# Group 9's gate logits as PE products, and the first slot's gathers behind that group's row store

## The chip, the cores and the metric

The kernel runs on one core of one Trainium2 chip. The metric is the device time of one execution in microseconds (us), the median of three runs; a profiled execution, from which the rows below come, is timed apart from these.

## What is computed

The reference has three stages. The first is a recurrent attention over 4 batches, 8 heads, 768 steps and a head size of 40:

```python
y[:, :, t] = np.einsum('bhd,bhde->bhe', rt, state)
Sa = np.einsum('bhde,bhe->bhd', state, at)
state = state * wt[:, :, None, :] - np.einsum('bhd,bhe->bhde', Sa, bt) + np.einsum('bhd,bhe->bhde', vt, kt)
```

Its result, 3072 tokens of 320 features, goes through a dense layer pair (320 to 2048 and back, with a leaky ReLU of slope 0.01). The last stage sends each token to one of 8 experts: the largest of 8 gate logits picks the expert, its softmax probability scales the result, and the expert is again a layer pair, 320 to 1024 and back with a ReLU. All is float32.

## The kernel before, in words

The attention is computed in 24 chunks of 32 steps. Two chunks of all batches make a group of 256 tokens, so there are 12 groups (0 to 11), and the dense layers work group by group behind the attention. A group has 16 steps, one for each 128 of the 2048 inner features, and each step is done in two halves: a call of `half` runs either layer 1 of a step (eight products into psH, line 716) or layer 2 of the step two before it (six products into psX, line 732). After layer 1 ScalarE (ACT) writes 0.01 of it to g (L720), VectorE (DVE) takes the maximum (L721), ACT rounds it to gh (L722), and GpSimd (POOL) subtracts to get the rest, gl (L723); layer 2 multiplies gh and gl. g has two buffers, gh and gl have three each.

When a group's layer 2 is complete, `route` (line 734) makes a list of pieces. The first, `take` (L750), copies the two token tiles (128 tokens each) from psX to the tile X, which has one buffer. From then on every call of `half` does one piece after its products. There are two forms of the logits. Groups below TURNED (line 36) take one DVE instruction for each expert and tile, 16 in all (L753, with weights in raws). From TURNED on a tile is transposed by TensorE (PE) in three pieces (`turn`, L759), copied by ACT (L760), multiplied by the gate weights on PE (`product`, L765) and copied by ACT again (L766); both tiles take 6 pieces. Then follow the maximum, the expert's code and the denominator (L772 to L793), the row store of X to the DRAM tensor x2d by SyncE (SP) (`fourth`, L797: two DMAs, of 128 rows with 385 numbers each), and two scatters of token numbers into a table by POOL (L810). A group's store comes 23 pieces after the first logit in the DVE form and 15 after it in the PE form. Some of a route's pieces do nothing, to keep a distance.

When the routes of group 8 and of group 9 are through, `early` (line 920) works out on DVE which experts have the fullest slots of 256 tokens: slots 0 and 1 after group 8, slot 2 after group 9 (EARLY, line 38). `fetch` (line 1055) then reads a slot's token numbers from the table (SP, L1063), adds two halves (POOL, L1070) and gathers the tokens' rows from x2d with two indirect DMAs on POOL (L1071) into xg. Loads of an expert's weights are five DMAs of SP into raw (L1049), which ACT and DVE split into two parts (L1091, L1092).

The kernel is scheduled by hand: each engine takes its instructions in the order in which the code emits them. Two strings of words set that order, one word for one thing to emit. The attention's strings end with the 336th call of `half`, 16 halves into group 10. From there the string TAIL (line 61) rules, read by `tail` (line 1422): H is one half of the dense layers with its routing piece, l one weight load, s one piece of the split, i the reads of the table for slots 0 and 1, t one step of their fetch (clearing xg, first gather, second gather, then the same for slot 1), x the transposes of slot 0. The framework puts a wait where two instructions touch the same tile or the same DRAM tensor; x2d counts as one tensor for gathers and stores alike.

Group 9's copy into X is in half 324 and its first logit piece too; group 10's copy is in half 356. TAIL's first H is half 337.

Of the kernel before, what the change touches and what calls it, by code (L numbers as in the profile page):

```python
# [22 lines left out]
B, H, S, D = 4, 8, 768, 40  # L23
# [9 lines left out]
CAP = NT + SL  # L33
NSLOT = NT // SL + E - 1
PACE = (2, 1), (2, 2), (2, 2)
TURNED = 10
FETCH = 1, 5
EARLY, NE = {9: (0, 1), 10: (2,)}, 3
LOAD, SPLIT = 18, 27
# [19 lines left out]
    "H H s1 H s2 w w H H H w H s6a.-1 s6b.-1 w s3x H H s3a w H s4a s4b H w H s5a s5b w l3.1 H H s3b H l2.1 H H w w H "  # L59
)  # L60
TAIL = (
    "i H l t H H H H t l l H t l H H H l H s H H H H H H s H H H H H H s H H t H H H t H t H H c s s H H H H s H H l H H H H H H H H s H H H s x s H l H l H "
    "l s l H H "
)
NFIX = NT // SL + E // 2
NTB = 8 * CAP + 8 * SL
# [439 lines left out]
class Moe1:  # L506
# [313 lines left out]
    def units(s):  # L820
# [3 lines left out]
        def second():  # L824
            g, f, gh, gl = lag.pop(0)
            s.layer2(f, gh, gl)
            if f == NF - 1:
                r = s.route([s.x2c[2 * g], s.x2c[2 * g + 1]], s.ids[:, 2 * g:2 * g + 2], g >= TURNED)
                r.pop(0)()
# [625 lines left out]
```

## Time and profile before

| what | us |
|---|---|
| median of three runs | 1109.37 |
| the runs | 1102.41, 1109.37, 1110.74 |
| profiled execution, its own time | 1101.14 |
| its span, first to last instruction | 1099.4 |
| PE busy in the span | 948.1 (86%) |
| DVE busy | 803.1 (73%) |
| ACT busy | 529.3 (48%) |
| POOL busy | 501.1 (46%) |
| mean granted clock of PE | 0.955 |

The span is cut by three stages: attention and dense layers together up to some 761 us, dense layers alone up to some 826 us, then the experts. PE is TensorE's products, PEld its weight loads. A row of the timeline gives the start, the busy time, the engine, the line, the operation with output and inputs, and in brackets how long the engine had been idle and what ended that. A row of waits gives who waited for whom, the total, how often, and the longest. In the tables of stretches each engine has its busy time and its count, then come the granted clock as a share of full speed, the busy share of the DMA engines and their GB/s.

### The profile page before, as it was taken

The page shows a single profiled execution, that of the slowest core. Times are in us where ns is not written, and L with a number is a line of the kernel's source. Part 1 is how long each engine was busy: PE and PEld are TensorE (multiplying, and loading weights), DVE is VectorE, ACT ScalarE, POOL GpSimd, SP SyncE. Part 2 cuts the span into 40 slices and gives each one's busy share as a digit, 9 for nine tenths or more (in the row PEclk, how much of TensorE's full clock was granted, in tenths as well). Part 3 has the DMA queues.
Part 4 walks back from the last instruction along what each step waited for, and adds up shares of the span by engine and source line. Part 5 has one row for each costly group of instructions (what it writes and reads, how often), then busy time and mean ns, then how long its engine had stood idle before and what let it go on. Part 6 is the DMA issues. An engine that isn't in the chain of part 4 may idle for free. (4 is left out here: it accounts for less than half of the span.)

```text
span 1099.4 us, 40716 instructions
## 1 busy us (share of the span) xinstructions
PE 948.1 (86%) x16853; PEld 893.9 (81%) x16853; DVE 803.1 (73%) x1882; ACT 529.3 (48%) x1316; POOL 501.1 (46%) x690
## 2 busy tenths in 40 slices
PE   3476788978899988889989999999798899999993
PEld 3366677768788887888889988998798899999993
DVE  8989787757778787868787767667447777777761
ACT  4545554653434444444435443444456466666650
POOL 5124145214873489447864595334456333233210
PEclk9999986878999999999999999999899999999997
DMA  7978776846445755564555432331425663732520
GB/s 249 241 223 224 213 209 177 222 132 194 134 123 161 163 158 160 163 167 125 151 150 151 117 81 81 82 91 48 149 87 159 168 178 111 236 109 70 173 91 17
DMA packets 132523, 163.20 MB, mean 148 GB/s; under 512 B 67851, under 2 KB 90011, under 8 KB 132199
## 3 DMA queue, kind: packets, MB, share of 16 engines
q1 hardware_dynamic: 122215, 141.31, 46.3%
q10 hardware_dynamic: 5760, 10.49, 3.3%
q0 software_dynamic: 4352, 8.69, 2.7%
q8 instruction: 135, 2.21, 0.9%
q14 instruction: 61, 0.50, 0.2%
HBM read 127.62 MB, written 42.27 MB: 155 GB/s over the span
## 5 line engine op out<-in xcount | busy, mean ns | idle before, releaser
L723 POOL TENSOR_TENSOR gl<-g,gh 128x256 fp32r<-128x256 f32 x192 | 155.3, 812 | 227.9 <-ACT gh L722 202.1
L721 DVE TENSOR_TENSOR g<-psH,g 128x256 f32<-128x256 f32 x192 | 81.1, 423 | 119.2 <-ACT g L720 117.5
L722 ACT CAST gh<-g 128x256 fp32r<-128x256 f32 x192 | 77.9, 406 | 166.3 <-DVE g L721 163.2
L732 PE MATMUL psX<-woh,gh 128*128 128x320 f32 x384 | 133.9, 349 | 2.0 <-ACT woh L643 1.1
L732 PE MATMUL psX<-woh,gl 128*128 128x320 f32 x384 | 124.2, 323 | 6.0 <-POOL gl L723 5.8
L720 ACT ACTIVATE g<-psH 128x256 f32<-128x256 f32 x192 | 73.5, 383 | 112.4 <-PE psH L716 87.5
L732 PE MATMUL psX<-wol,gh 128*128 128x320 f32 x384 | 123.2, 321 | 0.0
L264 PE MATMUL psA<-AtI,KB 40*64 40x72 f32 x1408 | 71.0, 264 | 34.7 <-DVE KB L243 18.5
L264 PEld LDWEIGHTS psA<-AtI,KB 40*64 40x64 f32 x1408 | 62.8, 166 | 41.1 <-POOL woh L242 18.5
L753 DVE SCALAR_TENSOR_TENSOR junk<-X,raws 128x320 bf16<-128x320 f32 x160 | 92.1, 576 | 5.0 <-ACT X L750 3.1
L716 PE MATMUL psH<-xh,wih 128*128 128x256 f32 x384 | 86.3, 308 | 4.4 <-DVE g L721 3.6
L732 PEld LDWEIGHTS psX<-woh,gl 128*128 128x128 f32 x384 | 76.1, 198 | 9.0 <-POOL gl L723 8.8
L304 POOL TENSOR_TENSOR itmp<-Tinv 128x30 f32<-128x30 f32 (+14 forms) x120 | 71.0, 592 | 25.4 <-DVE Tinv L296 18.2
L732 PEld LDWEIGHTS psX<-woh,gh 128*128 128x128 f32 x384 | 76.3, 199 | 7.5 <-ACT woh L643 1.3
L716 PE MATMUL psH<-xl,wih 128*128 128x256 f32 x384 | 80.6, 293 | 0.0
L716 PE MATMUL psH<-xh,wil 128*128 128x256 f32 x384 | 80.2, 292 | 0.0
L1155 POOL DMA_INDIRECT out<-ey,sid x32 | 32.4, 1011 | 105.0 <-ACT ey L1154 99.5
L732 PEld LDWEIGHTS psX<-wol,gh 128*128 128x128 f32 x384 | 76.7, 200 | 0.5 <-DVE wol L644 0.3
L310 POOL TENSOR_TENSOR Tinv<-Tinv,itmp 128x30 f32<-128x30 f32 (+14 forms) x120 | 71.8, 598 | 7.8
L716 PEld LDWEIGHTS psH<-xh,wih 128*128 128x128 f32 x384 | 65.9, 199 | 8.9 <-DVE g L721 5.5
L1133 DVE SCALAR_TENSOR_TENSOR ehl<-psH,ehh 128x256 fp32r<-128x256 f32 x86 | 36.2, 421 | 41.5 <-ACT ehh L1132 41.3
L1132 ACT ACTIVATE ehh<-psH 128x256 fp32r<-128x256 f32 x86 | 33.1, 384 | 64.9 <-PE psH L1129 62.7
(284 smaller groups left out, 2792.3 us busy)
## 6 DMA issues: line engine op xcount, KB each, us to landing
raw<-hwe SPq DMA_DIRECT2D x48, 512.0 KB
raw<-hwe SPq DMA_DIRECT2D x32, 640.0 KB
in<-h SPq DMA_DIRECT2D x23, 521.0 KB
KB<-h SPq DMA_DIRECT2D x22, 512.0 KB
L<-dKBr SPq DMA_DIRECT2D x24, 320.0 KB
dKBr<-KBr SPq DMA_DIRECT2D x22, 320.0 KB
lamY<-dl SPq DMA_DIRECT2D x24, 264.0 KB
dl<-lam SPq DMA_DIRECT2D x22, 264.0 KB
```

What stands on the lines that cost most here:

```text
L264: nc.tensor.matmul(v[64 * i:64 * i + 64, k, :], z["KB"][64 * i:64 * i + 40, p, :], z["AtI"][64 * i:64 * i + 40, p, :], start=True, stop=True)
L304: eng.tensor_tensor(out=box["v"], in0=T[:, k + 1:32, k:k + 1].to_broadcast([128, n, k]), in1=T[:, k:k + 1, 0:k].to_broadcast([128, n, k]), ...
L310: eng.tensor_tensor(out=T[:, k + 1:32, 0:k], in0=T[:, k + 1:32, 0:k], in1=box["v"], op=ALU.add)
L716: nc.tensor.matmul(ps[:, 0:256], w, x, start=(n == 0), stop=(n == 7))
L720: nc.scalar.activation(out=g, in_=ps[:, 0:256], func=AF.Copy, scale=0.01)
L721: nc.vector.tensor_tensor(out=g, in0=ps[:, 0:256], in1=g, op=ALU.max)
L722: nc.scalar.copy(out=gh, in_=g)
L723: return gh, gl, lambda: nc.gpsimd.tensor_tensor(out=gl, in0=g, in1=gh, op=ALU.subtract)
L732: nc.tensor.matmul(s.x2[t][:, 0:DM], x[:, o], w[:, f, :], start=(f == 0 and n == 0), stop=(f == NF - 1 and n == 2))
L753: nc.vector.scalar_tensor_tensor(out=s.junk, in0=X[:, t, 0:DM], scalar=1.0, in1=s.wg[:, e], op0=ALU.mult, op1=ALU.mult, accum_out=lg[:, t, ...
L1132: nc.scalar.activation(out=hh, in_=ps, func=AF.Relu)
L1133: nc.vector.scalar_tensor_tensor(out=hl, in0=ps, scalar=0.0, in1=hh, op0=ALU.max, op1=ALU.subtract)
```

## The change

Two constants change; no function does.

```diff
-TURNED = 10
+TURNED = 9
 TAIL = (
-    "i H l t H H H H t l l H t l H H H l H s H H H H H H s ...
+    "i H l t H H H H l l H l H H t H H t l s H H H H H H s ...
...
-    "l s l H H "
+    "l H l s l H H "
```

The strings break at another place, so that a word has gone from the end of the one line to the start of the next; all words behind the second gather (the third t) keep their order, as do the counts of H, l, s and t. With TURNED at 9 group 9 uses the PE form. Its route is 8 pieces shorter: the store is emitted with half 339 (347 before), the scatters with halves 340 and 343 (348 and 351), and the work of `early` for slot 2 with half 343 (351). The two gathers of slot 0 come after halves 344 and 346 (341 and 342 before). So they stood ahead of group 9's store and now stand behind it, by 5 and 7 halves, or by 8 and 10 words of TAIL that are not t.

On PE the transposes of group 9's first tile come in at half 324, behind the group's last layer-2 products (psX) and ahead of the next layer-1 products (psH); X is the tile that ACT copies from psX.

```order
 L732 MATMUL psX_12816<-wol,gh 128x320
 L732 MATMUL psX_12816<-woh,gl 128x320
+L759 MATMUL psA<-ident,X_13678 128x128 x3
 L716 MATMUL psH<-xh,wih 128x256 x2
 L716 MATMUL psH<-xh,wis 128x256
```

One row is new here, and the layer-1 products of the next step stand behind it.

On SP this is the place from group 11's input (xl) to the first expert's weights (raw); X_13678 is group 9's X.

```order
 L693 DMA xl<-xT_88 64x256
 L694 DMA xl<-xT_88 64x256
+L797 DMA x2d<-X_13678 4x32x385 x2
 L1049 ISA
 L1049 DMA raw<-hwe 128x1024
```

The store stood behind the four weight loads that follow here, next to group 10's store, and is now ahead of them.

On POOL this is the stretch from the clearing of slot 0's xg to that of slot 1's; tbl_90 and tbl_91 are the two halves of the table.

```order
 L1075 MEMSET xg 128x770
 L723 TENSOR_TENSOR gl<-g,gh 128x256 x2
-L1070 TENSOR_TENSOR sid<-sid_14024 128x2
+L810 DMA tbl_90<-ids,dst 28672x1
+L723 TENSOR_TENSOR gl<-g,gh 128x256
+L810 DMA tbl_91<-ids,dst 28672x1
+L723 TENSOR_TENSOR gl<-g,gh 128x256
+L1070 TENSOR_TENSOR sid<-sid_14037 128x2
 L1071 DMA xg<-x2d,sid 128x385
 L723 TENSOR_TENSOR gl<-g,gh 128x256
 L1071 DMA xg<-x2d,sid 128x385
```

The scatters of group 9 were behind the gathers and are ahead of them; two more subtractions gl come ahead of the first gather.

## Rows read from the trace of the kernel before

**Rows 1.** Busy time by stretch: us, then PE, PEld, DVE, ACT, POOL, clock, DMA, GB/s.

```profile
700.00:750.00 50.00, 50.00 (x1058) 46.78 (x1057) 34.42 (x115) 21.09 (x54) 16.41 (x20) 1.00 0.34 90
750.00:800.00 50.00, 42.87 (x490) 40.74 (x490) 27.84 (x91) 22.47 (x59) 22.02 (x27) 0.93 0.29 91
```

**Rows 2.** Timeline of PE around group 10's copy: start, us, what, idle time before.

```profile
791.96 0.90 PE L759 MATMUL psH<-ident,X 128*128 128x128 f32 x3 [5.77 <-ACT X L750]
...
795.81 0.73 PE L765 MATMUL psH<-none,raws 128*128 128x8 f32 x6
796.39 0.48 PE L716 MATMUL psH<-xh,wih 128*128 128x256 f32 x2
...
798.63 0.46 PE L716 MATMUL psH<-xh,wih 128*128 128x256 f32 x2
...
801.18 0.40 PE L716 MATMUL psH<-xh,wih 128*128 128x256 f32 x2
...
803.02 0.40 PE L716 MATMUL psH<-xh,wih 128*128 128x256 f32 x2
```

**Rows 3.** Timeline of PE around group 9's copy.

```profile
749.34 0.40 PE L716 MATMUL psH<-xh,wih 128*128 128x256 f32 x2
...
751.57 0.66 PE L451 MATMUL psA<-ident,Xq 128*128 128x128 f32 x4 [0.34 <-ACT Xq L421]
753.07 0.41 PE L732 MATMUL psX<-woh,gh 128*128 128x320 f32 x1 [0.85 <-ACT X L750]
```

**Rows 4.** Timeline of ACT at group 10's copy.

```profile
791.48 0.76 ACT L750 COPY X<-psX 128x320 f32<-128x320 f32 x2 [3.98 <-DMA x2d<-X]
```

**Rows 5.** Timeline of SP (what it issues) from 769 to 782 us.

```profile
769.23 0.33 SPq L1049 DMA_DIRECT2D raw<-hwe  x1
...
770.67 0.59 SPq L694 DMA_DIRECT2D xl<-xT  x1
771.48 1.99 SPq L1049 DMA_DIRECT2D raw<-hwe  x4
781.16 1.33 SPq L797 DMA_DIRECT2D x2d<-X  x2
```

**Rows 6.** Waits of SP from 760 to 845 us: total, times, longest.

```profile
SPq L797 <- DMA xg<-x2d,sid: 40.6, 4, 26.6
```

**Rows 7.** Busy time by stretch, columns as in rows 1.

```profile
790.00:795.00 5.00, 3.04 (x14) 3.04 (x15) 0.00 (x0) 1.57 (x4) 0.00 (x0) 0.50 0.04 11
795.00:800.00 5.00, 5.00 (x40) 4.94 (x39) 1.54 (x3) 2.41 (x8) 1.69 (x3) 0.94 0.00 0
```

**Rows 8.** Timeline of PE at group 11's first transposes.

```profile
826.06 0.55 PE L759 MATMUL psH<-ident,X 128*128 128x128 f32 x3 [0.41 <-ACT X L750]
```

**Rows 9.** DVE's groups by line from 752 to 772 us: busy, mean ns, idle before.

```profile
L753 DVE SCALAR_TENSOR_TENSOR junk<-X,raws 128x320 bf16<-128x320 f32 x16 | 8.1, 506 | 1.0 <-ACT X L750 0.8
```

**Rows 10.** Timeline of ACT at group 9's copy.

```profile
752.60 0.75 ACT L750 COPY X<-psX 128x320 f32<-128x320 f32 x2
```

**Rows 11.** Timeline of PE: an earlier gap of similar length.

```profile
302.93 0.92 PE L408 MATMUL psA<-Xq,NT 32*32 32x40 f32 x64 [3.71 <-ACT Xq L413]
```

**Rows 12.** Busy time of the stretch behind that gap, columns as in rows 1.

```profile
304.00:308.00 4.00, 3.56 (x75) 3.47 (x76) 1.35 (x3) 1.11 (x3) 3.63 (x5) 0.57 0.55 159
```

**Rows 13.** Timeline of SP: an earlier group's store, and the issue that waited for it.

```profile
595.95 1.26 SPq L797 DMA_DIRECT2D x2d<-X  x2
...
607.54 0.51 SPq L282 DMA_DIRECT2D Pq<-Ms  x1
```

**Rows 14.** Timeline of POOL from 774 to 777 us.

```profile
774.69 1.02 POOL L1071 DMA_INDIRECT xg<-x2d,sid  x1 [0.32 <-issue]
775.74 1.47 POOL L723 TENSOR_TENSOR gl<-g,gh 128x256 fp32r<-128x256 f32 x2
```

**Rows 15.** Timeline at the layer-2 unit of half 350.

```profile
779.55 0.31 PE L732 MATMUL psX<-woh,gl 128*128 128x320 f32 x1
```

More of the change, by code (lines that the diff above doesn't have):

```diff
@@ L61 @@
 TAIL = (
-    "i H l t H H H H t l l H t l H H H l H s H H H H H H s H H H H H H s H H t H H H t H t H H c s s H H H H s H H l H H H H H H H H s H H H s x s H l H l H "
-    "l s l H H "
+    "i H l t H H H H l l H l H H t H H t l s H H H H H H s H H H H H H s H H t H H H t H t H H c s s H H H H s H H l H H H H H H H H s H H H s x s H l H "
+    "l H l s l H H "
 )
```

## The prediction

> **What bounds the kernel now.** I read the table of stretches first: for each 50 us it gives the busy time of every engine. Between 700 and 750 us TensorE (PE) is busy for the whole stretch, between 750 and 800 us for 42.87 of 50 [rows 1]. The 7.13 us that are missing there are the place of this change. The timeline of PE names them: one gap of 5.77 us that ends at 791.96 with group 10's first transposes, waiting for ScalarE's (ACT's) copy into X [rows 2], and two of 0.34 and 0.85 us at 751.57 and 753.07 [rows 3]. Together that is 6.96 of the 7.13 us. Outside these gaps PE is full, so it sets the pace of the stage, and what another engine saves there is worth nothing.
>
> The big gap is then followed back. ACT began these copies at 791.48 after 3.98 us in which it waited for a DMA, x2d<-X [rows 4]: X is a single buffer, and group 10 may not be copied into it before group 9's row store has read it. The timeline of SyncE (SP) has that store issued at 781.16 [rows 5]; it lands about 10.3 us later (791.48 less 781.16). SP's own waits say why it was issued so late: row stores waited 40.6 us in all for the first slots' gathers [rows 6], because the gathers read the tensor that the store writes. So the chain is gather, store, copy, transposes, PE.
>
> After the gap the granted clock is 0.50 from 790 to 795 us and 0.94 in the next 5 us [rows 7]: the lower of the two levels (1.2 GHz), after an idle PE.
>
> **The change, term by term.** The sum is made against the profiled execution (1101.14 us, of which the span is 1099.4).
>
> *The old wait goes: -5.36 us.* Group 9's route is now 8 pieces shorter ahead of the store, so the store comes 17 halves before group 10's copies instead of 9, ahead of four weight loads on SP and ahead of the gathers on GpSimd (POOL). It will have landed long before. What is late next is the copy itself: group 11's transposes show a wait of 0.41 us for it, with no store in the way [rows 8]. So 5.77 - 0.41. The other end is 3.98 us, ACT's own idle time: had ACT been let go, it would have begun at 787.5, after casts that VectorE (DVE) had delayed while it worked out the third slot. That work, done when group 9's route is through, moves 8 halves earlier too, so I take 5.36.
>
> *The clock is kept: -1.61 us.* At the low clock three transposes, one layer-1 unit and one layer-2 unit took 795.81 - 791.96 = 3.85 us; the same set at full clock 798.63 - 796.39 = 2.24 us [rows 2].
>
> *PE products: +2.22 us.* A layer-1 and a layer-2 unit alone take 803.02 - 801.18 = 1.84 us. With one turn they take 2.24, with one product 801.18 - 798.63 = 2.55 [rows 2]. Per token tile that is 0.40 + 0.71, and there are two tiles. PE is full, so all of it counts.
>
> *DVE's relief: 0.* The sixteen logits and their accumulator reads go, 8.1 us for the first [rows 9]. They stand beside a full PE, and none of the three gaps was ended by them. ACT's four small copies are added beside the same PE.
>
> *A new wait at the first turn: +2.54 us.* The first transposes of group 9 now stand directly behind the last layer-2 unit of that group on PE, where the next layer-1 unit began at 749.34 [rows 3]. They need ACT's copy of X, and ACT began it only at 752.60 [rows 10]; PE was released by it at 753.07. Nothing in the change moves ACT's work ahead of that copy. So PE, which used that time for a layer-1 unit and two attention units, stands from 749.34 to 753.07, 3.73 us; the waits of 0.34 and 0.85 us that it had in this stretch fall away. Behind the transposes on PE stand all of the two stages' products. Below: 0.41 us, the wait of group 11, if ACT should be early; that makes it -0.78.
>
> *The clock there: +1.6 us.* A gap of 3.71 us that ended at 302.93 was followed by a mean clock of 0.57 from 304 to 308 us [rows 11, 12]. A gap of nearly the same length is added, and I take the loss just measured. The other end is 0.
>
> *A new wait at the first gather: +4.1 us.* The gather now stands 5 halves behind the store and must wait until it has landed. SP comes to the store at about 771.3: it follows the loads of xl, the last of which was issued at 770.67 [rows 5], and is ready by then, 8 halves earlier than before. Landing is taken at 10.3 us as above; another store, with four loads issued behind it, went out at 595.95, and an issue that waited for it came at 607.54 [rows 13], 11.6 us later. So the gather starts at 781.6. Then come its own 1.02 us, some 0.3 us, and one subtraction gl of 0.74 us [rows 14]: 783.7. PE wants that gl at the third layer-2 product of two steps later (half 350), in the trace at 779.55 [rows 15]. The delay is 4.1 us. Behind the waiting gather on POOL stand the subtractions of all later steps; the second gather, one step on, finds the store landed and costs POOL a further 1.0 us, which its slack takes. With 11.6 us it is 5.4; if the store has landed when POOL arrives, 0. (The times are those of the old trace. The later PE in the terms above shifts SP and POOL alike, since SP's part begins with the store of the last attention chunk, which waits for PE.)
>
> *The clock there: +1.6 us*, as after the gap of 3.71 us [rows 11, 12], or 0.
>
> *Moved at no cost.* SP issues the four loads of the first expert 1.33 us later (the duration of the store's two issues) [rows 5]; the first two splits read the piece ahead of the store. The table scatters come ahead of the gathers on POOL, which has idle time there.
>
> Sum: -5.36 - 1.61 + 2.22 + 2.54 + 1.6 + 4.1 + 1.6 = +5.1 us.
>
> **A rule beside it.** In the changed order SP issues the store behind one weight load and the loads of xl, and ahead of four more; SP is through with the loads ahead of it at 771.3 [rows 5]. The Trainium skill ("DMA: Bandwidth & Descriptors", section "Queues, rings and completion order") says that each DMA engine takes a queue's descriptors in ring order, and that a completion is signalled after every earlier write of that engine. By that the four loads behind the store don't hold it, and the sum stays +5.1; if they did, the third rival's time below would come. No run here shows a store in exactly this place.
>
> **Rivals.**
> 1. *The store has landed when POOL gets there* (not slower). For it: SP's issue may come earlier than I read it, and POOL has idle time. Against: 10.3 and 11.6 us for two stores, and only 5 halves, of 0.92 us each by the 1.84 us above. The last two terms fall away: 5.1 - 4.1 - 1.6 = -0.6.
> 2. *Neither wait opens* (faster). ACT is early at the first turn too: -5.36 - 1.61 + 2.22 - 0.78 = -5.5. Against it: the copy at 752.60 hangs on ACT's and DVE's queues, which the change leaves alone ahead of it.
> 3. *The store lands only with the weight loads* (slower still). In the trace the loads went out from 769.23 on, and the second gather, issued at 774.69 [rows 14], was through only when SP let the store go at 781.16: 11.9 us after the first load. With the store's 1.33 us that makes 784.5 for the landing instead of 781.6, so 5.1 + 2.9 = +8.0.
>
> That the change doesn't do what it says is excluded by the order of PE and SP.
>
> **How the numbers follow.** The three runs shown lie at 1102.41, 1109.37 and 1110.74 us, the profiled one at 1101.14; a difference of about 1% (11 us) is what a measurement of this kernel can tell from no change. The profiled time is 8.2 us under the median, and four times so far apart give no better base than their mean, 1105.9. On it the forecast is 1105.9 + 5.1 = 1111.0; on the median of the runs it would be 1114.5. Rival 1 gives 1105.3, rival 2 1100.4, rival 3 1113.9. Chances: forecast 0.48, rival 1 0.25, rival 2 0.10, rival 3 0.12, something else 0.05. The range, 1100 to 1118, has rival 2 at its lower end; the upper one is the forecast on the median, with 11.6 us for the landing and some scatter. Within 1% are the forecast, rival 1 and most of the others: 0.83. Over 1% slower come rival 3 and the forecast where the scatter adds to it, 0.12; over 1% faster rival 2 with the scatter, 0.05.
>
> **What would show it.** In the changed kernel's profile: the gap of 5.77 us ahead of group 10's transposes gone, and no ACT wait for x2d<-X; a new PE gap of 3 to 4 us ahead of group 9's first transposes; POOL waiting for x2d<-X at its first gather, and about 4 us of PE waiting for gl two steps on; a clock below 1.00 after each. If POOL doesn't wait there, the sixth term is wrong; if the first transposes wait under 1 us, the fourth. A PE that is full from 750 to 800 us would make the forecast wrong altogether.

## The result and the profile after

| | kernel before | changed kernel |
|---|---|---|
| median, us (9 runs of each) | 1102.24 | 1113.77 |
| lowest to highest | 1098.56 to 1110.74 | 1109.05 to 1118.55 |
| profiled execution, own time / span | 1101.14 / 1099.4 | 1116.35 / 1114.7 |
| mean granted clock of PE | 0.955 | 0.945 |

The ratio is 1.0086, with an interval of 1.0059 to 1.0113: slower by 0.86%, or 1102.24 x 0.0086 = 9.5 us (the two medians lie 11.5 us apart), where the forecast was +5.1 us and 1111.0 us in all. The sign is as forecast and the size is about double. (Ratios leave out runs more than 1.5% above the fastest of their kernel.)

Totals are blurred by what goes on elsewhere in the program, so one stretch is compared throughout: from the start of group 9's last layer-2 unit on PE to that of group 11's. It holds all that the change touches. The timeline of PE of the changed kernel has its two ends and what stood in between (start, busy us, engine, line, operation, and the idle time before it with what ended that):

```profile
750.38 0.31 PE L732 MATMUL psX<-woh,gh 128*128 128x320 f32 x1
...
754.99 0.90 PE L759 MATMUL psA<-ident,X 128*128 128x128 f32 x3 [3.57 <-ACT X L750]
...
759.52 0.62 PE L732 MATMUL psX<-woh,gh 128*128 128x320 f32 x1
...
795.33 0.64 PE L732 MATMUL psX<-woh,gl 128*128 128x320 f32 x1 [4.03 <-POOL gl L723]
...
805.23 0.55 PE L759 MATMUL psH<-ident,X 128*128 128x128 f32 x3 [0.87 <-ACT X L750]
...
836.24 0.31 PE L732 MATMUL psX<-woh,gh 128*128 128x320 f32 x1
```

Before, its two ends were:

```profile
748.46 0.31 PE L732 MATMUL psX<-woh,gh 128*128 128x320 f32 x1
...
824.60 0.31 PE L732 MATMUL psX<-woh,gh 128*128 128x320 f32 x1
```

The stretch is 836.24 - 750.38 = 85.9 us; before, it is 824.60 - 748.46 = 76.1 us. So 9.7 us are lost inside it, as much as the ratio tells. The two profiled executions lie further apart: their spans differ by 15.2 us, of which 1.9 lie ahead of the stretch and 3.6 behind it; on these see the two kernels once more. The gap of 5.77 us [rows 2] has become 0.87 us, and two gaps of 3.57 and 4.03 us are new. ACT confirms both readings: its copy for group 10 no longer waits for x2d<-X (3.98 us before [rows 4]), and group 9's copy comes no earlier than before [rows 10].

```profile
754.52 0.75 ACT L750 COPY X<-psX 128x320 f32<-128x320 f32 x2
...
804.76 0.75 ACT L750 COPY X<-psX 128x320 f32<-128x320 f32 x2
```

The second gap is followed back through POOL and SP. POOL stood 5.95 us at the first gather, and one subtraction gl came behind it. The table names raw<-hwe as what ended that wait; what the gather needs is the row store, which SP had issued at 781.34, 12.1 us earlier (compare [rows 5, 14]). In the kernel with the filled wait below the same wait bears the name x2d<-X.

```profile
781.34 1.30 SPq L797 DMA_DIRECT2D x2d<-X  x2
782.86 3.30 SPq L1049 DMA_DIRECT2D raw<-hwe  x4
```

```profile
793.48 1.05 POOL L1071 DMA_INDIRECT xg<-x2d,sid  x1 [5.95 <-DMA raw<-hwe]
794.55 0.73 POOL L723 TENSOR_TENSOR gl<-g,gh 128x256 fp32r<-128x256 f32 x1
```

The total of SP's waits hides the change: its row stores still wait 42.2 us in all for gathers, 40.6 before [rows 6]. Of the 40.6 only 7.5 us were group 9's store; 26.6 were group 10's and 6.4 group 11's. Now group 9's store waits for no gather, and the 42.2 are group 10's (34.3) and group 11's (7.9), which end no wait of PE in the stretch. A total of waits doesn't say which of them counts.

```profile
SPq L797 <- DMA xg<-x2d,sid: 42.2, 4, 31.0
```

The table of stretches (columns as in [rows 1]) shows what the two gaps alone do not:

```profile
700.00:750.00 50.00, 49.99 (x1119) 46.68 (x1118) 33.86 (x109) 21.76 (x55) 17.41 (x20) 1.00 0.35 94
750.00:800.00 50.00, 42.29 (x444) 40.12 (x443) 18.22 (x61) 18.65 (x49) 15.90 (x22) 0.81 0.36 92
...
750.00:755.00 5.00, 1.43 (x12) 1.17 (x10) 2.38 (x10) 2.74 (x8) 1.03 (x2) 0.85 0.09 17
755.00:760.00 5.00, 5.00 (x33) 4.70 (x34) 0.42 (x1) 2.27 (x7) 1.15 (x2) 0.50 0.02 3
760.00:765.00 5.00, 5.00 (x24) 5.00 (x24) 0.03 (x1) 1.61 (x4) 0.00 (x0) 0.50 0.12 41
765.00:770.00 5.00, 5.00 (x151) 4.63 (x151) 2.26 (x6) 1.17 (x3) 0.73 (x1) 0.78 0.02 3
...
790.00:795.00 5.00, 1.30 (x11) 1.03 (x9) 1.74 (x3) 1.14 (x3) 1.50 (x2) 0.95 0.88 268
795.00:800.00 5.00, 4.67 (x19) 4.67 (x20) 0.85 (x2) 1.72 (x5) 2.78 (x5) 0.50 0.67 132
800.00:805.00 5.00, 4.36 (x29) 4.09 (x27) 1.65 (x3) 2.10 (x6) 1.47 (x3) 0.87 0.00 1
```

PE is busy for 42.29 of the second 50 us, hardly less than the 42.87 before [rows 1], but at a clock of 0.81 instead of 0.93: busy time alone hides the loss. There are two levels, 1.00 and 0.50, so a mean of 0.85 over 5 us means that (1 - 0.85) / 0.5 x 5 = 1.5 us were at the low one. Behind the first gap this gives 1.5 + 5 + 5 + 2.2 = 13.7 us, although PE has no gap from 755 on. Behind the second it is 0.5 + 5 + 1.3 = 6.8 us.

### The profile page after: what moved, and what is told of

Same layout as the page of the kernel before. It is cut to its first block, busy times and chain, and to the rows that moved or that the text cites. A ratio compares the mean times of both kernels' runs of the same rounds, so it can differ in the third digit from the quotient of the medians.

```text
span 1114.7 us, 40724 instructions
## 1 busy us (share of the span) xinstructions
PE 962.9 (86%) x16871; PEld 908.6 (82%) x16871; DVE 792.8 (71%) x1850; ACT 529.7 (48%) x1320; POOL 501.9 (45%) x690
## 5 line engine op out<-in xcount | busy, mean ns | idle before, releaser
L723 POOL TENSOR_TENSOR gl<-g,gh 128x256 fp32r<-128x256 f32 x192 | 152.7, 798 | 239.3 <-ACT gh L722 214.6
L732 PE MATMUL psX<-woh,gl 128*128 128x320 f32 x384 | 126.3, 329 | 10.4 <-POOL gl L723 10.3
L732 PEld LDWEIGHTS psX<-woh,gl 128*128 128x128 f32 x384 | 77.2, 201 | 13.7 <-POOL gl L723 13.3
L753 DVE SCALAR_TENSOR_TENSOR junk<-X,raws 128x320 bf16<-128x320 f32 x144 | 83.5, 580 | 4.0 <-ACT X L750 2.3
L716 PEld LDWEIGHTS psH<-xl,wih 128*128 128x128 f32 x384 | 64.5, 206 | 0.3 <-DVE xl L701 0.3
```

The costliest lines, as they stand in the source:

```text
L716: nc.tensor.matmul(ps[:, 0:256], w, x, start=(n == 0), stop=(n == 7))
L723: return gh, gl, lambda: nc.gpsimd.tensor_tensor(out=gl, in0=g, in1=gh, op=ALU.subtract)
L732: nc.tensor.matmul(s.x2[t][:, 0:DM], x[:, o], w[:, f, :], start=(f == 0 and n == 0), stop=(f == NF - 1 and n == 2))
L753: nc.vector.scalar_tensor_tensor(out=s.junk, in0=X[:, t, 0:DM], scalar=1.0, in1=s.wg[:, e], op0=ALU.mult, op1=ALU.mult, accum_out=lg[:, t, ...
```

## The experiments

"Low" in the table is the time at the low clock behind group 9's first transposes (before: behind its copy), by the sum above. The waits are PE's: at group 9's first transposes, for gl at the first gather, and at group 10's first transposes; where the second column says none, the waits of 0.34 and 0.85 us of before [rows 3] are all there is. The expert stage runs from the first expert's first layer-1 product to the end of the span. All times in us.

| kernel | stretch | wait, group 9 | low | wait for gl | wait, group 10 | expert stage | ratio to before (interval) |
|---|---|---|---|---|---|---|---|
| before | 76.1 | none | 0 | none | 5.77 | 273.1 | 1 |
| before, again | 76.9 | none | 0 | none | 6.79 | 275.5 | 0.9988 (0.9960 to 1.0016) |
| changed | 85.9 | 3.57 | 13.7 | 4.03 | 0.87 | 276.7 | 1.0086 (1.0059 to 1.0113) |
| changed, again | 85.2 | 3.58 | 10.3 | 4.87 | 0.87 | 276.6 | 1.0071 (1.0043 to 1.0100) |
| gathers later | 77.1 | 3.57 | 6.8 | 0.54 | 0.85 | 277.1 | 1.0031 (1.0000 to 1.0062) |
| transposes one half later | 80.6 | 2.61 | 3.4 | 5.21 | 0.87 | 276.4 | 1.0063 (1.0022 to 1.0103) |
| both | 76.5 | 2.62 | 3.4 | 1.17 | 0.78 | 276.3 | 1.0024 (0.9993 to 1.0055) |
| wait filled with products | 80.8 | filled | 0 | 5.53 | 0.87 | 273.0 | 1.0022 (0.9991 to 1.0053) |
| logits alone | 90.3 | 3.57 | 13.6 | 8.43 | 0.87 | 276.8 | 1.0132 (1.0084 to 1.0180) |
| gathers' move alone | 78.8 | none | 3.4 | none | 6.69 | 275.3 | 1.0032 (0.9999 to 1.0064) |
| gathers behind a later store, logits on DVE | 74.3 | none | 3.4 | none | 2.54 | 276.4 | 0.9944 (0.9915 to 0.9973) |
| transposes two halves later, gathers later | 73.2 | none | 0 | none | 1.31 | 276.9 | 0.9985 (0.9956 to 1.0014) |
| the same, group 10 one half later | 72.1 | none | 0 | none | 0.36 | 277.0 | 0.9979 (0.9954 to 1.0004) |
| the last once more | 75.6 | none | 3.4 | none | 0.36 | 277.2 | 0.9971 (0.9943 to 1.0000) |

### The gathers later

The gathers' words move behind halves 351 and 352 (seven and six halves on, not five and seven as the expectation has it).

```diff
-    "i H l t H H H H l l H l H H t H H t l s H H H H H H s ...
+    "i H l t H H H H l l H l H H H H l s H H H H H t H s t ...
```

> The changed kernel with slot 0's two gathers five and seven halves further on, so that group 9's store has long landed when POOL comes to them. The stretch meant below runs on PE from the last layer-2 unit of group 9 to that of group 11: 76.1 us before, 85.9 us after the change. Theory (the two waits, each with its low clock, cost what the kernel lost): POOL's 5.95 us at the first gather and PE's 4.03 us for gl go, and with them the low clock behind it, so the stretch falls by 6.6 us (what PE fell back between half 348 and half 351) to 79.3 us; the total goes from about +10 us against the kernel before to about +4. The wait of 3.57 us at the first transposes and the 13.7 us of low clock behind it stay. Rival (the gathers only pass a lag on, PE then waits for something else there, or the expert stage is late because xg comes late): the stretch stays above 83 us, or the total doesn't fall.

The wait for gl is 0.54 us, and the stretch 77.1 us, 2.2 less than the theory gave. The excess has a source that I had not reckoned with, ahead of the edit: up to group 9's logits the instructions of this kernel are those of the changed one, PE's wait is the same, and yet the clock came back earlier.

```profile
754.98 0.90 PE L759 MATMUL psA<-ident,X 128*128 128x128 f32 x3 [3.57 <-ACT X L750]
```

```profile
750.00:755.00 5.00, 1.43 (x12) 1.17 (x10) 2.37 (x10) 2.75 (x8) 1.04 (x2) 0.96 0.04 12
755.00:760.00 5.00, 5.00 (x33) 4.70 (x34) 0.42 (x1) 2.28 (x7) 1.13 (x2) 0.50 0.01 3
760.00:765.00 5.00, 5.00 (x115) 4.81 (x115) 0.42 (x1) 2.38 (x6) 0.42 (x1) 0.86 0.12 41
```

From 760 to 765 us the clock is 0.86 here and 0.50 in the changed kernel: 6.8 us at the low level instead of 13.7. The length of the low clock is not fixed by the instructions, nor by the wait ahead of them.

### The first transposes one half later

```diff
-            by = [lambda: turn(0), rest, lambda: product(0), lambda: turn(1), rest, lambda: product(1)]
+            by = [rest] * (turned - 1) + [lambda: turn(0), rest, lambda: product(0), lambda: turn(1), rest, lambda: product(1)]
...
-                r = s.route([s.x2c[2 * g], s.x2c[2 * g + 1]], s.ids[:, 2 * g:2 * g + 2], g >= TURNED)
+                r = s.route([s.x2c[2 * g], s.x2c[2 * g + 1]], s.ids[:, 2 * g:2 * g + 2], (g >= TURNED) + (g == 9))
```

> The changed kernel with group 9's first transposes one half later, behind the next layer-1 products and the attention's products (its whole route is one piece longer, the store one half later). Theory: the wait of 3.57 us at the first transposes goes back to the two short waits of before (0.34 and 0.85 us), the clock stays at 1.00, and the stretch on PE from group 9's last layer-2 unit to group 11's falls by 2.4 + 4.7 = 7.1 us to about 79 us (up to 80 if the later store makes the gather wait longer); the total falls to about +3 us against the kernel before. Rival (the products for the logits and what they displace cost the time, not the wait): only the 2.4 us of the wait go, 83.5 us, with the clock still low behind the transposes.

A miss in the wait: it fell by 0.96 us only.

```profile
764.05 0.55 PE L759 MATMUL psA<-ident,X 128*128 128x128 f32 x3 [2.61 <-ACT X L750]
764.53 0.83 PE L498 MATMUL psA<-ident,Vx 40*80 40x40 f32 x16
765.29 0.66 PE L451 MATMUL psA<-ident,Xq 128*128 128x128 f32 x4
```

The layer-1 products had moved ahead of the transposes, but the attention's (L498, L451) still stood behind them; my expectation had put them ahead. The low clock is nevertheless 3.4 us instead of 13.7, and the way from group 9's last unit to the unit of half 350 takes 35.2 us against 40.5. The whole stretch, 80.6 us, lies over the theory's 79 to 80, with PE waiting 5.21 us for gl. So the rival is out as well: more than the wait's part has gone, and the added products stayed.

### Both

The two diffs above together.

> Both edits, later gathers and later first transposes. Theory: the two effects add, so the stretch on PE from group 9's last layer-2 unit to group 11's is 85.9 - 6.6 - 7.1 = 72.2 us, 3.9 us less than before the change (-5.4 - 1.6 + 2.2 = -4.8 by the prediction's terms), and the total is 3 to 5 us under the kernel before, if the expert stage is as it was. Rival for the rest (the change also costs 3 to 4 us in the expert stage, by the earlier store or the later gathers): the total is no better than that of the kernel before although the stretch is 72.

76.5 us instead of 72.2: of the 4.3 us, 2.62 - 1.19 = 1.4 are what is left of group 9's wait, 1.2 the wait for gl, and the clock, low for 3.4 us behind the first wait and at 0.66 from 800 to 805 us, is left for the rest. The total is not below that of before, as the stretch isn't.

### The wait filled with products

```diff
             ps = box[t] = s.bank()
+            if warm and t == 0:
+                for _ in range(16):
+                    nc.tensor.matmul(ps.rearrange("q (a b) -> q a b", a=4), s.ones, s.ones[:, None, :].to_broadcast([128, 4, 128]), start=True, stop=True)
```

> The changed kernel with sixteen products of 512 columns, whose result is overwritten, put on PE ahead of group 9's first transposes: they fill the time in which PE stands there (16 x 0.21 us at full clock, by 0.15 us for 320 columns), nothing else is changed. Theory (PE's standing still lets the clock fall, and 4.7 us of the loss at this place are the low clock): the granted clock stays at 1.00 behind the transposes, the stretch falls by about 4.7 us to 81 us, and the total by as much. Rival (the clock falls for the work that comes then, small transposes and attention products, or the loss there is another): the clock is low from 754 to 767 us as in the changed kernel, and the stretch stays at 86 us.

The products fill 3.63 us, as long as PE had stood, and the first transposes follow without a gap:

```profile
754.61 3.63 PE L760 MATMUL psA<-ones 128*128 128x512 bf16 x16
758.34 0.55 PE L762 MATMUL psA<-ident,X 128*128 128x128 f32 x3
```

```profile
755.00:760.00 5.00, 4.90 (x33) 2.80 (x30) 0.91 (x2) 3.10 (x9) 1.37 (x2) 1.00 0.06 14
760.00:765.00 5.00, 5.00 (x68) 4.76 (x70) 0.85 (x2) 3.42 (x10) 0.74 (x1) 1.00 0.10 34
```

The clock stays at 1.00, and the way to the unit of half 350 takes 35.1 us instead of 40.5: 5.4 us less, with the transposes as far behind group 9's last unit as in the changed kernel (4.61 us). That is the price of the low clock by itself, from one profile, measured by an edit that does nothing else. It also shows that the work that follows does not bring the clock down. The stretch is 80.8 us, as the theory has it. Part of the gain is given back at the gather, where PE waits 5.53 us instead of 4.03. PE is there 5.4 us earlier and the store is issued as much earlier (25.6 us after group 9's last unit instead of 31.0), but the gather starts 13.6 us after that issue instead of 12.1.

```profile
792.95 1.05 POOL L1074 DMA_INDIRECT xg<-x2d,sid  x1 [7.44 <-DMA x2d<-X]
```

### The logits alone, and the gathers' move alone

First TURNED at 9 with the words of TAIL as they were, then TURNED at 10 with the new words.

```diff
-TURNED = 10
+TURNED = 9
```

> The first half of the change alone: group 9's logits on PE, the words of TAIL as they were, so the store keeps its new place on SP but the gathers come after halves 341 and 342, two subtractions gl (some 3 halves) nearer to it. Theory (the gather waits for a landing that is set by SP's store, so POOL stops as much longer as it comes earlier): POOL waits some 8 us at the first gather instead of 5.95, PE 6 to 7 us for gl instead of 4.03, and the stretch from group 9's last layer-2 unit to group 11's is 2 to 3 us longer than in the changed kernel. Rival (the gathers' place is of no matter): the same waits.

```profile
797.41 1.04 POOL L1071 DMA_INDIRECT xg<-x2d,sid  x1 [9.41 <-DMA raw<-hwe]
```

```profile
799.27 0.64 PE L732 MATMUL psX<-woh,gl 128*128 128x320 f32 x1 [8.43 <-POOL gl L723]
```

POOL waited 9.41 us instead of 5.95, PE 8.43 instead of 4.03. The direction is the theory's; the size is over it, since the gather started only 797.41 - 784.57 = 12.8 us after the store's issue. Without the second half of the change the first would have cost 14.2 us in the stretch (90.3 less 76.1), so the gathers' move is worth some 4 to 5 us beside the logits.

```diff
 TURNED = 10
...
-    "i H l t H H H H t l l H t l H H H l H s H H H H H H s ...
+    "i H l t H H H H l l H l H H t H H t l s H H H H H H s ...
```

> The second half of the change alone: group 9's logits stay on DVE (its store behind half 347), the gathers come three and four halves later than before, still ahead of that store. Theory (gather, store, copy and transposes are one chain): the store goes out some 3 us later and group 10's first transposes wait 8 to 10 us for ACT's copy instead of 5.8 (6.8 in the second profile of before); the stretch on PE from group 9's last layer-2 unit to group 11's grows by 2 to 4 us to 78 to 81 us; no wait at group 9's own logits. Rival (the store's time is set by SP's queue or by group 9's logits on DVE, not by the gathers): the wait stays at 6 to 7 us and the stretch at 76 to 77 us.

```profile
790.00 1.33 SPq L797 DMA_DIRECT2D x2d<-X  x2
```

```profile
800.06 0.76 ACT L750 COPY X<-psX 128x320 f32<-128x320 f32 x2 [4.66 <-DMA x2d<-X]
```

The store comes 790.00 - 754.12 = 35.9 us after group 9's last unit, 32.7 before: 3.2 us later, as the chain asks. PE's wait grew by 0.9 us only, to 6.69 us, which misses the theory's 8 to 10 us and lies in the rival's range, since PE itself was 2.0 us later there, with 3.4 us of low clock from 755 to 765 us. The store's own 3.2 us and the stretch of 78.8 us speak for the theory: the store is tied to the gathers, and alone this half only lengthens the old chain.

### The gathers behind a later store, the logits on DVE

TURNED at 10, the gathers behind halves 357 and 358; the store stays behind half 347.

```diff
-    "i H l t H H H H t l l H t l H H H l H s H H H H H H s H H H H H H s ...
+    "i H l t H H H H l l H l H H H H l s H H H H H H s H H H H H t H s t ...
```

> Group 9's logits stay on DVE, and slot 0's gathers come behind halves 357 and 358, behind that group's store (half 347), which then waits for no gather. Theory: the store goes out behind its half at PE's time of group 10's thirteenth layer-2 unit, about 3 to 4 us earlier against PE than before, lands 10 to 13 us later, and group 10's first transposes wait 1 to 4 us instead of 5.8 to 6.8; no products are added, so the stretch from group 9's last layer-2 unit to group 11's is 71 to 74 us. Rival (the four weight loads that stand ahead of the store on SP hold its landing): the wait stays over 5 us and the stretch at 75 us or more.

```profile
786.56 1.33 SPq L797 DMA_DIRECT2D x2d<-X  x2
```

```profile
798.32 0.76 ACT L750 COPY X<-psX 128x320 f32<-128x320 f32 x2 [0.79 <-DMA x2d<-X]
```

The store goes out 786.56 - 757.08 = 29.5 us after group 9's last unit, 3.2 us earlier than before, and ACT waits 0.79 us for it instead of 3.98. The stretch is 74.3 us. The four loads ahead of the store did not hold it: the copy that waits for it began 11.8 us after its issue. The ratio has to be read with care: one run of this kernel, 1093.58 us, lies 7.7 us under its next and decides which of its runs count; over all its runs the median is 1106.64 us against 1108.92, or 0.2% less, which is what the stretch would give.

### The transposes two halves later

Two rests ahead of group 9's first transposes, which puts them behind the layer-2 unit that came next on PE before the change; the gathers behind halves 352 and 354. The `by` line is that of the transposes one half later.

```diff
+                r = s.route([s.x2c[2 * g], s.x2c[2 * g + 1]], s.ids[:, 2 * g:2 * g + 2], (g >= TURNED) + 2 * (g == 9))
...
+    "i H l t H H H H l l H l H H H H l s H H H H H H t s H H t H H H H s ...
```

> The changed kernel with group 9's first transposes two halves later (behind the layer-1 products, the attention's products and the layer-2 unit that came next on PE before the change) and slot 0's gathers behind the 6th and 8th half after the sixteenth's place, still further from the store. Theory: no long wait is left at either place, the clock stays at 1.00 from 745 to 800 us, and the stretch on PE from group 9's last layer-2 unit to group 11's is 76.1 - 4.9 (5.77 less 0.87, group 10's transposes) - 1.6 + 2.2 = 71.8 us, some 4 us under that of the kernel before; by the total 0.4% faster than before, less than the other runs' scatter of a single time. Rival (ACT's copy of X is late for whatever stands next on PE, here the layer-2 unit that needs psX): a wait of 2 us or more moves to that unit, with a low clock behind it, and the stretch is 75 us or more.

No long wait and no low clock are left at either place; 73.2 us, 1.4 over the theory, of which 1.31 - 0.87 = 0.4 is at group 10's transposes, 0.54 at the first gate product and 0.27 beside the gathers. The next kernel has group 10's transposes one half later too, and the gathers behind halves 357 and 358:

```diff
+                r = s.route([s.x2c[2 * g], s.x2c[2 * g + 1]], s.ids[:, 2 * g:2 * g + 2], (g >= TURNED) + 2 * (g == 9) + (g == 10))
...
+    "i H l t H H H H l l H l H H H H l s H H H H H H s H H H H H t H s t ...
```

> As the run with group 9's first transposes two halves later, with the gathers behind halves 357 and 358 and group 10's first transposes one half later too. Theory: the waits left at group 10's copy (1.31 us) and beside the gathers (0.27 us) go, so the stretch from group 9's last layer-2 unit to group 11's falls from 73.2 to about 72 us. Rival (ACT's copy or the later logits make PE wait at another place): 73 us or more.

```profile
753.09 0.31 PE L732 MATMUL psX<-woh,gh 128*128 128x320 f32 x1
...
757.72 0.41 PE L732 MATMUL psX<-woh,gh 128*128 128x320 f32 x1 [0.85 <-ACT X L750]
...
761.58 0.83 PE L765 MATMUL psA<-none,raws 128*128 128x8 f32 x6 [0.56 <-ACT raws L760]
...
795.31 0.55 PE L759 MATMUL psH<-ident,X 128*128 128x128 f32 x3 [0.36 <-ACT X L750]
...
825.19 0.31 PE L732 MATMUL psX<-woh,gh 128*128 128x320 f32 x1
```

825.19 - 753.09 = 72.1 us, with no wait over 0.85 us between. Its time was taken twice:

> The last version once more, for its time. Theory: the stretch from group 9's last layer-2 unit to group 11's is 72 us again, 4 to 5 us under that of the kernel before, and the expert stage is as long as there (275 to 277 us); so its time is 0.3 to 0.4% under that of the kernel before, and with the first timing together the difference is told from none. Rival (what is gained in the stretch is lost behind it): the same time as the kernel before although the stretch is 72 us.

Here PE stopped once in the middle of an attention step, for 1.79 us without a releaser, and the clock was low for 3.4 us behind that; the stretch is 75.6 us, not the 72 of the theory. What stopped PE is not shown. In the trace's DMA packets a 16 KB packet of the instruction queue starts 0.9 us behind this step's first product, where it started 3.2 us ahead of it in the other profile of the same kernel; that it is the cause was not tried.

```profile
766.94 0.27 PE L463 MATMUL psA<-Rr,Vt 40*32 40x32 f32 x9 [1.79 <-issue]
```

The ratios are 0.9979 and 0.9971. If the two are taken as independent, with half widths of 0.0025 and 0.0028, their mean is 0.9975, give or take 0.0019: faster than before by a quarter of a per cent, and only just told from none.

### The two kernels once more

> The kernel before once more, for a second profile of it. In its first profile the expert stage (first layer-1 product of the first expert to the end of the span) takes 273.1 us, in those of the changed kernel and of its variants 276.3 to 277.1. Theory (the change costs nothing there, the 3.6 us are scatter of a chain of DMAs ahead of the third and fourth slot): some 276 us this time, with the wait for xg longer than the 0.95 us of the first profile, and 76.1 us again from group 9's last layer-2 unit to group 11's. Rival (the change costs 3 to 4 us in the expert stage): 273 us again.

```profile
797.45 0.90 PE L759 MATMUL psH<-ident,X 128*128 128x128 f32 x3 [6.79 <-ACT X L750]
```

The stretch is 76.9 us, with the gap 1.0 us longer, and the expert stage 275.5, between the theory's 276 and the first profile's 273.1. What bears on it most is the kernel with the filled wait: it has the whole change, and its expert stage is 273.0 us. The longest wait there is for the gather of a later slot, at the end of a chain of DMAs. It is 3.14 us in the changed kernel and 1.67 with the filled wait; the kernel before has both sizes as well, 1.68 us in its first profile and 3.07 in its second. In the ten other profiles it is 3.1 to 4.2 us.

```profile
889.77 0.30 PE L1112 MATMUL epx<-ident,xg 128*128 128x128 f32 x1 [3.14 <-DMA xg<-x2d,sid]
```

```profile
885.51 0.30 PE L1115 MATMUL epx<-ident,xg 128*128 128x128 f32 x1 [1.67 <-DMA xg<-x2d,sid]
```

```profile
875.61 0.30 PE L1112 MATMUL epx<-ident,xg 128*128 128x128 f32 x1 [1.68 <-DMA xg<-x2d,sid]
```

```profile
881.98 0.30 PE L1112 MATMUL epx<-ident,xg 128*128 128x128 f32 x1 [3.07 <-DMA xg<-x2d,sid]
```

So the change need not cost anything there. That it does so in some executions, by a microsecond or two, stays open with two profiles of before.

> The changed kernel once more. Theory: the same two waits (3.57 us at the first transposes, 4 us for gl two steps after the first gather) to within 0.3 us; the clock behind the first is low for between 6 us (as in the run with later gathers, whose instructions there are the same) and 14 us (as in the first profile), so the stretch from group 9's last layer-2 unit to group 11's is 83 to 86 us. Rival (the low clock of 13.7 us belongs to this order of instructions): 85.9 us again, to within 0.5.

The first wait is the same to 0.01 us, the second 0.84 us longer, and the low clock 0.83 for 5 us, then 0.50 and 0.64, so 1.7 + 5 + 3.6 = 10.3 us: between the two others, and no property of the order of instructions. The stretch is 85.2 us.

## Why the prediction was right in kind and too small

The stretch can be cut at the units of halves 350 and 356 (the first and the last of the stage at the gather; on PE 779.26 and 785.14 us before, 790.84 and 803.31 after). PE fell back by 9.7 us up to the first, by 6.6 us in between, and won 6.5 us from there on. Beside the prediction's terms:

| term | predicted | measured | from |
|---|---|---|---|
| old wait goes | -5.36 | -4.90 | 0.87 left of 5.77 |
| clock kept | -1.61 | -1.6 | 6.5 less 4.9 |
| PE products | +2.22 | +2.2 to 2.4 | see below |
| new wait at the first turn | +2.54 | +2.38 | 3.57 less 0.34 and 0.85 |
| clock there | +1.6 | +5.1 | 9.66 - 2.38 - 2.22 |
| new wait at the first gather | +4.1 | +4.03 | the gap for gl |
| clock there | +1.6 | +2.6 | 6.59 less 4.03 |
| sum | +5.1 | +9.7 | the stretch |

**The old wait and its clock: right.** What was late next was the copy, at 0.87 us instead of the 0.41 taken from group 11.

**The PE products: right.** In the last kernel of the table, in its first profile, which has no long wait, the way to the unit of half 350 is 33.8 us, 3.0 more than the 30.8 before, and 0.56 of that is a wait for raws: 2.4 us. In the changed kernel's own row of the table they are taken as forecast, 2.22.

**DVE's relief at nothing: nothing speaks against it.** DVE's busy time in the 50 us from 750 fell from 27.84 [rows 1] to 18.22 us, in part because PE got less far in them, and no part of the sum is missing that it would have to explain.

**The wait at the first turn: right,** and for the reason given. ACT's copy did not move, and PE stood before it.

**The clock there: this is the step that failed.** The prediction said "I take the loss just measured", 1.6 us, from the one gap whose recovery it had timed. That priced a low clock by one execution of another place. The two gaps that the prediction had before it were followed by less: 3.4 us by [rows 12], and 6.8 us at group 10's gap, of which 3.2 lay in the wait. Here the low clock lasted 13.7 us, 10.3 and 6.8 in three executions with the same wait ahead of it, and took 5.1, 4.2 and 2.5 us from PE, worked out in the same way (way to the unit of half 350 of 40.46, 39.64 and 37.88 us, each less 30.80, 2.22 and the wait). The filled wait shows that the term is what it was called: with PE kept busy 5.4 us come back. The Trainium skill ("TensorE: Matmul & The Clock Gate", section "HAM oscillation — how this bites in real kernels") counts half of the time at the lower clock as lost. Of the 13.7 us some 1.5 lay in the wait itself, so that would be 6.1 us; the trace has 5.1, a little less. The rule tells the price once the length is known, and the length is what I had wrong.

**The wait at the first gather: right, partly by luck.** I had the store issued at 771.3 in the old trace's time and landing 10.3 us later, so 781.6. The gather started 12.1 us after the issue, but the store was issued earlier as seen from PE: 781.34 less the 11.58 us by which PE had fallen back is 769.8. PE had lost time to the low clock and SP not as much of it. The two errors leave 781.9, and the clock's price there was 1.0 us over the forecast. Of the 12.1 us the store took 11.2: the last of its semaphore updates in the trace is at 792.58. POOL then took another 0.9 before the gather started, as it did in four more profiles (1.2 us in a fifth), where ACT's copies began 0.1 us after theirs; the forecast had taken its landing from such a copy. The prediction's reading of the 40.6 us of store waits [rows 6] was too wide: group 9's store has 7.5 of them.

**The rivals.** The first (store landed when POOL comes) and the second (no wait opens) fell with POOL's 5.95 and PE's 3.57 us. The third had the landing at 784.5, held by the weight loads; 781.9 is the forecast's. The rule that stood beside it, from the Trainium skill ("DMA: Bandwidth & Descriptors", section "Queues, rings and completion order"), had these loads not holding the store. The trace agrees: the store's last update at 792.58 comes ahead of the last one of each of the four loads behind it (793.55 to 799.16), and the same holds in the nine other profiles with loads right behind the store. Still, in six of the ten a gather that waited for the store started 12.1 to 13.6 us after its issue, and in the four profiles without such loads ACT's waiting copy began after 10.1 to 11.8. By the store's last update the two groups are at 11.2 to 12.7 and 10.0 to 11.7 us, so 0.9 us or more of the difference is POOL's start, and what is left overlaps. And with the transposes two halves later, with the same four loads right behind the store, its last update came after 7.6 to 7.8 us in three profiles. So the loads alone don't make a store late; what sets its landing stays open.

**The base.** The forecast's 1105.9 us lies 3.7 over the median of before beside these runs, and under the 1107 to 1110 us that the kernel before took beside the experiments. That the 1111.0 us came within 3 us of 1113.77 owes as much to this as to the terms.

The two halves of the change each paid one chain for another. The logits on PE bought an early store with a wait at the first turn, and the gathers, put behind that store, then waited for it to land. Both new waits were matters of place: two halves for the transposes and eight to thirteen for the gathers take them away, and what then remains of the change is a stretch 4 us shorter than before.

## What to carry to other kernels

Price a new wait of an engine that sets the pace with its clock, as a range and not as one number: a wait of 3.6 us brought 7 to 14 us of half clock here, which cost 0.7 to 1.4 times the wait itself on top of it. When a consumer is moved behind a store to break a chain, count the store's landing in steps of the program and move it that far; when a first step reads a copy that another engine makes, put the work that used to cover the copy back in between. To tell a lost clock from lost work, fill the wait with products that nobody reads and see what comes back.

## What the runs showed of the hardware

- The low clock that came with one and the same wait of 3.57 us lasted 6.8, 10.3, 13.6 and 13.7 us in four executions whose instructions there are alike. Up to 1.5 us of it lay in the wait; behind the wait PE had no gap at all.
- It can also fall after less: the waits of some 0.34 and 0.85 us at group 9's copy left the clock at 1.00 in both profiles of before, and were followed by 3.4 us of low clock in two kernels with the same order of instructions there (from 760 to 765 us 0.70 in the one, 0.75 in the other).
- A row store of 256 rows, a bare 1.3 us to issue, took 10.1 to 13.6 us until what waited for it went on; in three profiles in which nothing waited, the store's last semaphore update came after 7.6 to 7.8 us. POOL's gather started 0.9 to 1.2 us after that update, ACT's copy 0.1 us.
- PE stopped once for 1.79 us in a run of 128 products, without a wait that the profile shows.
- The expert stage of programs that are alike there took 273.0 to 277.2 us. In the two shortest PE waited 1.7 us for a later slot's gather, in all others 3.1 to 4.2 us.
